# Moving batch 1's attention work by one step beside the output products of block 0 (linear attention followed by a gated feed-forward layer)

## The chip, the cores and the metric

The kernel runs on one core of one Trainium2 chip. The metric is the device time of one execution in microseconds (us). The profile of one execution gives a span that is about 1.8 us shorter than the device time of the same execution; positions inside a profile are told in us from the start of its span. The profile's short names for the engines are PE (tensor engine, matrix products), PEld (its weight loads), DVE (vector engine), ACT (scalar engine), POOL and SP (in this stretch they mainly issue loads and stores; POOL also takes a power for the norm).

## The reference

Eight batches of linear attention with 8 heads, 576 tokens and head width 64, and after it a layer with a root-mean-square norm and a gated product on all 4608 tokens:

```python
q_p = phi(q, cos_w, sin_w)           # relu(q) times cos and sin of the position, 128 wide
k_p = phi(k, cos_w, sin_w)
kv  = einsum('bhsf,bhsd->bhfd', k_p, v)
z   = sum(k_p, axis=2)
num = einsum('bhsf,bhfd->bhsd', q_p, kv)
den = einsum('bhsf,bhf->bhs', q_p, z) + 1e-06
x   = num / den                      # as [4608, 512]

xn  = x / sqrt(mean(x * x) + 1e-06) * rms_g
g   = xn @ w_gate                    # 512 -> 1536
out = (silu(g) * (xn @ w_val)) @ w_out
```

## The kernel before

The feed-forward layer is cut into blocks of 512 tokens. A block has twelve "slots" (one per 128 columns of the hidden width, each with a gate and a value product, a Silu on ACT and a product on DVE) and then its output products. The attention of batch b+1 is woven between the feed-forward products of block b. The order of instructions on each engine is the order of the program text; the kernel places every piece by hand.

This is about the end of block 0, where all four output products run side by side in four banks of PSUM, over twelve steps of the hidden width, and batch 1 is prepared between the steps. What is done for batch 1:

- **phi of k and q**: relu with a scale, half of each on DVE and half on ACT.
- **q transposes** (`q_tr`): PE transposes phi of q for 128 tokens, and DVE or ACT copies the result to SBUF.
- **k-z-v** (`kvz`): the product of phi of k with v and a column of ones (72 small products into psA), then two copies to SBUF.
- **n-d** (`nd`): numerator and denominator for 128 tokens, 8 products into psA. `nd_post` divides on DVE and so frees psA; `x_sq` (ACT) and a power on POOL give the norm's factor; `x_norm` (DVE) applies it; `tr1` transposes the result on PE, and ACT copies it. Then block 1 can use these 128 tokens.

```python
    for j in range(NJ):                                  # NJ = 9
        at(0, 8 + j // 4, "post", k_phi, V, 1, j, 0)     # DVE half, slots 8, 9, 10
        at(0, 8 + j // 4, "post", k_phi, A, 1, j, 1)     # ACT half
    for c in range(2):
        at(0, 10 + c, "post", q_phi, V, 1, c, 0)
        at(0, 10 + c, "post", q_phi, A, 1, c, 1)
    # ... slots 6 to 11 of block 0 ...
    banks0 = [psC[0][:, :], psC[1][:, :], psG[0][:, :], psG[1][:, :]]
    nd_at = {4: 0, 6: 1, 8: 2, 9: 3}
    for n in range(NNT - 2):                             # NNT = 12: steps 0 to 9
        if n == 3:
            kvz_pe(1, psA); kvz_evac(A, 1, psA, 0); kvz_evac(V, 1, psA, 1)
        if 1 <= n <= 4:
            c = n - 1
            q_tr_pe(1, c, qbank[c]); q_tr_evac(V if c < 2 else A, 1, c, qbank[c])
        if n == 0:
            ...                                          # q_phi for c = 2, 3
        if n == 1:
            v_cast(A, 1, *LOW); v_cast(V, 1, *HIGH)
        # ... loads for batch 2 ...
        if n == 7: x_norm(1, 0)
        if n == 9:
            x_norm(1, 1); tr1(0, psV[0][:, :])
        if n in nd_at:
            j = nd_at[n]
            nd_pe(1, j, psA); nd_post(1, j, psA); x_sq(1, j)
        for j in range(4):
            out_mm(0, j, n, banks0[j])
    x_norm(1, 2)
    tr1(1, psV[1][:, :])
    for j in (2, 3):
        for n in (NNT - 2, NNT - 1):
            out_mm(0, j, n, banks0[j])
    out_store(V, 0, 2, banks0[2]); out_store(A, 0, 3, banks0[3])
    for j in (0, 1):
        ...                                              # steps 10 and 11 of the others
    gval_mm(1, 0, 0, (0, 256))      # block 1's first product, into psG[0] and psV[0]
    ...                             # third and fourth xn transposes, stores, slot 1
    for n in range(2):
        gval_mm(1, n, n, (256, 512))                     # "second half" of slots 0 and 1
```

The fourth output product of step 0 goes into psG[1], which is free only when ACT has read slot 11's gate product there (its Silu). And the weights of the output product (`wo`) come in four loads of three steps; the second, for steps 3 to 5, is issued by POOL only when q of batch 1 has landed.

## Time and profile before

| | before |
|---|---|
| device time, median of 3 runs | 328.78 us (328.71 to 329.32) |
| PE busy | 318.9 us of a span of 327.9 us (97%) |
| DVE and ACT busy | 57% and 54% |
| granted PE clock | 1.00 |

The profile is of one more execution, which took 329.70 us.

PE is nearly always at work, so a reorder without a change of work can only win or lose PE's idle time. The table by windows says where that is; its columns after the window are its length, the busy time and instruction count of PE, PEld, DVE, ACT and POOL, the granted clock, the DMA share and GB/s.

```profile
38.00:62.00 24.00, 22.51 (x247) 13.70 (x246) 17.76 (x43) 17.41 (x36) 4.68 (x7) 1.00 1.06 287
62.00:327.00 265.00, 261.69 (x1839) 125.53 (x1836) 143.52 (x302) 135.87 (x280) 15.39 (x28) 1.00 0.59 143
```

In the 24 us that the change touches PE is idle for about 1.5 us by this account. A 128x512 product is recorded as 0.38 us long, but when PE is full such products start 0.216 us apart, so a record reaches about 0.16 us into the idle time behind it. The Trainium skill, "Perfetto Trace Analysis", section "Summary: the profiler window per engine type", says that the end of a PE record is an estimate; this trace agrees (0.38 against 0.216 us). So idle time is measured here from start to start: what lies between two starts, less 0.216 us for each 128x512 product in it. Here are lines of PE's timeline of the kernel before (start, duration, engine, line, operation, output and inputs, array and shape, count; in brackets the idle time by the records, and who ended it):

```profile
39.64 1.02 PE L426 MATMUL psG<-xnT,wg 128*128 128x512 bf16 x4 [0.25 <-ACT sg L435]
...
41.79 0.38 PE L446 MATMUL psG<-wo,hT 128*128 128x512 bf16 x1
43.20 0.38 PE L446 MATMUL psG<-wo,hT 128*128 128x512 bf16 x1 [1.03 <-ACT sg L435]
...
54.22 0.39 PE L412 MATMUL psV<-ident,xn 128*128 128x128 bf16 x4
54.73 0.40 PE L310 MATMUL psA<-kvzs,qpT 128*128 128x65 bf16 x8
...
56.93 1.03 PE L446 MATMUL psC<-wo,hT 128*128 128x512 bf16 x4
57.79 0.60 PE L426 MATMUL psG<-xnT,wg 128*128 128x256 bf16 x4
...
60.31 0.61 PE L426 MATMUL psG<-xnT,wg 128*128 128x256 bf16 x4
```

From start to start, slot 11 lost 0.42 us at 39.64, and the fourth product of step 0 lost 1.19 us at 43.20, both waiting for a Silu (sg). Further back there is little: the four transposes at 54.22 take 0.22 us, so the fourth n-d (54.73) waited about 0.29 us, and block 1's first product (57.79) follows the four products at 56.93 without a gap. The second half of block 1's slots starts at 60.31.

ACT's timeline of the kernel before, with the same columns, shows why the Silus are late:

```profile
37.40 1.71 ACT L209 ACTIVATE kpm<-rk,tab 128x256 bf16<-128x256 f32 x4 [1.70 <-DMA rk<-in_k_dram]
39.01 0.57 ACT L435 ACTIVATE sg<-psG 128x512 f32<-128x512 f32 x1
39.49 1.69 ACT L209 ACTIVATE kpm<-rk,tab 128x256 bf16<-128x256 f32 x4
41.08 0.58 ACT L435 ACTIVATE sg<-psG 128x512 f32<-128x512 f32 x1
41.56 0.50 ACT L209 ACTIVATE kpm<-rk,tab 128x256 bf16<-128x256 f32 x1
41.96 0.71 ACT L209 ACTIVATE qp<-rq,tab 128x512 bf16<-128x512 f32 x1
42.57 0.58 ACT L435 ACTIVATE sg<-psG 128x512 f32<-128x512 f32 x1
```

k of batch 1 lands at 37.40. From then on ACT works without a pause: nine k phis (kpm), one q phi (qp) and three Silus, and the last of these releases the product at 43.20.

### The profile page before, as it was taken

To read this page: it belongs to the slowest core of one execution; us is meant where nothing else is said; L and a number is where in the kernel's file an instruction comes from. 1 tells how busy PE (TensorE), PEld (TensorE's weight loads), DVE (VectorE), ACT (ScalarE), POOL (GpSimd) and SP (SyncE) were. 2 spreads that over 40 slices of the span, in tenths; PEclk is the share of its full clock that TensorE was granted. 3 is DMA by queue.
4 is the path that set the end of the run, shared out by engine and by line. 5 is a ranking of instruction groups with operands and counts; after the bars stand their busy time and mean duration, and the time that the engine had idled before them with its cause. 6 is when DMAs were issued, how large, how long until landed. Compare 5 with 4: busy or idle time off the path is not lost.

```text
span 327.9 us, 6438 instructions
## 1 busy us (share of the span) xinstructions
PE 318.9 (97%) x2441; PEld 161.0 (49%) x2441; DVE 185.9 (57%) x412; ACT 176.5 (54%) x366; POOL 32.1 (10%) x67
## 2 busy tenths in 40 slices
PE   7999989999999999999999999999999999999994
PEld 2488455654445444544454445444544444444442
DVE  6775577777755875578257745773577133203310
ACT  6864575875566457645654576456644233223321
POOL 1660022001100110011001100110011000000000
PEclk9999999999999999999999999999999999999999
DMA  7999999998969866975598569957621400020014
GB/s 260 217 186 224 371 165 333 325 172 198 252 187 171 209 185 170 222 206 159 186 222 193 148 187 224 197 166 210 130 49 32 130 32 0 28 102 1 0 34 96
DMA packets 80337, 53.91 MB, mean 164 GB/s; under 512 B 51377, under 2 KB 67761, under 8 KB 80306
## 3 DMA queue, kind: packets, MB, share of 16 engines
q1 hardware_dynamic: 73264, 48.64, 57.8%
q0 software_dynamic: 6880, 4.72, 10.0%
q8 instruction: 19, 0.31, 0.4%
q10 hardware_dynamic: 162, 0.13, 0.2%
q14 instruction: 12, 0.10, 0.1%
HBM read 37.75 MB, written 9.44 MB: 144 GB/s over the span
## 4 chain that ended last, share of the span: by engine, by line
PE 83%; DMA 8%; ACT 4%; DVE 1%; issue 1%; SPq 1%; POOL 0%; ACTq 0%
PE psC L446 26%; PE psG L426 24%; PE psV L426 24%; DMA rk<-in_k_dram 3%; PE psA L282 3%; DMA wv<-in_moe_w_val_dram 3%; DMA rv<-in_v_dram 2%; PE psA L310 2%; ACT kpm L209 2%; PE psG L446 1%; ACT sg L435 1%; PE psC L826 1%; PE psV L254 1%; ACT qp L209 0%; PE psA L317 0%
## 5 line engine op out<-in xcount | busy, mean ns | idle before, releaser
L441 DVE TENSOR_TENSOR hT<-psV,sg 128x512 bf16<-128x512 f32 x102 | 70.3, 689 | 97.4 <-PE psV L426 84.9
L435 ACT ACTIVATE sg<-psG 128x512 f32<-128x512 f32 x102 | 60.6, 594 | 65.9 <-PE psG L426 65.8
L426 PE MATMUL psG<-xnT,wg 128*128 128x512 bf16 (+1 forms) x368 | 92.9, 375 | 0.3 <-ACT sg L435 0.2
L426 PE MATMUL psV<-xnT,wv 128*128 128x512 bf16 (+1 forms) x368 | 92.7, 374 | 0.0
L446 PE MATMUL psC<-wo,hT 128*128 128x512 bf16 x396 | 89.6, 379 | 0.0
L426 PEld LDWEIGHTS <-wv 128*128 128x128 bf16 x416 | 40.7, 98 | 47.4
L446 PEld LDWEIGHTS <-hT 128*128 128x128 bf16 x420 | 40.2, 98 | 46.4
L426 PEld LDWEIGHTS <-wg 128*128 128x128 bf16 x416 | 38.6, 98 | 41.7 <-issue 0.5
L263 ACT COPY osb<-psC 128x512 f32<-128x512 f32 (+1 forms) x33 | 19.2, 582 | 41.0 <-PE psC L446 39.7
L380 POOL TENSOR_TENSOR rs<-ms,mhalf 128x1 f32<-128x1 f32 x36 | 19.9, 551 | 200.2 <-ACT scr L375 200.2
L387 DVE SCALAR_TENSOR_TENSOR xn<-xt,rs,gb 128x512 bf16<-128x512 f32 x36 | 26.8, 745 | 14.7 <-POOL rs L380 14.7
L375 ACT ACTIVATE scr<-xt 128x513 bf16<-128x513 f32 x36 | 22.9, 635 | 21.4 <-DVE xt L364 21.2
L209 ACT ACTIVATE kpm<-rk,tab 128x256 bf16<-128x256 f32 (+1 forms) x78 | 31.8, 477 | 3.5 <-DMA rk<-in_k_dram 3.5
L364 DVE TENSOR_TENSOR xt<-psA,rec 128x512 f32<-128x512 f32 x35 | 24.2, 691 | 1.2
L211 DVE TENSOR_SCALAR kpm<-rk,tab 128x256 bf16<-128x256 f32 (+1 forms) x84 | 22.1, 329 | 3.0 <-DMA rk<-in_k_dram 3.0
L209 ACT ACTIVATE qp<-rq,tab 128x512 bf16<-128x512 f32 x32 | 22.5, 714 | 0.2 <-DMA rq<-in_q_dram 0.2
L211 DVE TENSOR_SCALAR qp<-rq,tab 128x512 bf16<-128x512 f32 x32 | 15.1, 484 | 0.5 <-DMA rq<-in_q_dram 0.5
L310 PEld LDWEIGHTS <-qpT 128*128 128x128 bf16 x248 | 11.6, 98 | 6.7 <-issue 0.3
L310 PE MATMUL psA<-kvzs,qpT 128*128 128x65 bf16 x248 | 12.8, 194 | 0.2
L426 PE MATMUL psV<-xnt_tail,wv 128*128 128x512 bf16 x48 | 12.3, 379 | 0.0
L426 PE MATMUL psG<-xnt_tail,wg 128*128 128x512 bf16 x48 | 12.3, 379 | 0.0
L282 PEld LDWEIGHTS <-kpm 64*128 64x128 bf16 x576 | 9.9, 95 | 3.8 <-issue 2.7
(89 smaller groups left out, 168.4 us busy)
## 6 DMA issues: line engine op xcount, KB each, us to landing
out_dram<-osb SPq DMA_DIRECT2D x32, 256.0 KB, 2.5
rv<-in_v_dram SPq DMA_DIRECT2D x21, 288.0 KB, 3.2
rk<-in_k_dram SPq DMA_DIRECT2D x20, 288.0 KB, 3.5
rq<-in_q_dram SPq DMA_DIRECT2D x20, 256.0 KB, 3.4
rk<-in_k_dram SPq DMA_DIRECT2D x2, 1152.0 KB, 8.8
rq<-in_q_dram SPq DMA_DIRECT2D x2, 1024.0 KB, 11.4
rv<-in_v_dram SPq DMA_DIRECT2D x3, 576.0 KB, 10.4
wo<-in_moe_w_out_dram POOLq DMA_DIRECT2D x4, 384.0 KB, 7.0
```

The source lines that it names most:

```text
L209: nc.scalar.activation(out=out_ap, in_=in_ap, func=AF.Relu, scale=scale)
L211: eng.tensor_scalar(out=out_ap, in0=in_ap, scalar1=scale, scalar2=0.0, op0=ALU.mult, op1=ALU.max)
L282: nc.tensor.matmul(banks[c][:, r * E : (r + 1) * E], lhsT=kp_main[b][lo : lo + 64, j, r, :], rhs=vvm[b % 2][lo : lo + 64, r, j, :], start= ...
L310: nc.tensor.matmul(o[:, g, i, :], lhsT=qpT[(b, 0)][:, h, j * P : (j + 1) * P], rhs=kvz_of(b, h), start=True, stop=True,)
L364: nc.vector.tensor_tensor(out=xt[:, 0:DM].rearrange("p (b h d) -> p b h d", b=2, d=D), in0=o[:, :, :, 0:D], in1=rec[:, :, :].unsqueeze(3). ...
L375: nc.scalar.activation(out=scr[:, :], in_=xt[:, 0 : DM + 1], func=AF.Square, scale=1.0 / math.sqrt(DM), accum_out=ms[:, :],)
L380: nc.gpsimd.tensor_tensor(out=rs[:, :], in0=ms[:, :], in1=mhalf[:, :], op=ALU.pow)
L387: nc.vector.scalar_tensor_tensor(out=xn[:, :], in0=x_of[(b, j)][:, 0:DM], scalar=rs_of[(b, j)][:, :], in1=gb[:, :], op0=ALU.mult, op1=ALU. ...
L426: nc.tensor.matmul(pst[bank][:, cols[0] : cols[1]], lhsT=w[:, t, n * P : (n + 1) * P], rhs=x[:, t, cols[0] : cols[1]], start=(t == 0), sto ...
L435: nc.scalar.activation(out=sg[:, :], in_=psG[bank][:, :], func=AF.Silu)
L441: nc.vector.tensor_tensor(out=hTs[blk][:, n, :], in0=psV[bank][:, :], in1=sg[:, :], op=ALU.mult)
L446: nc.tensor.matmul(bank, lhsT=hTs[blk][:, n, j * P : (j + 1) * P], rhs=wo[:, n, :], start=(n == 0), stop=(n == NNT - 1),)
```

## The change

It takes one q phi out of the way of the last Silu, spreads the k phis as three per slot, and in return moves the q transposes and k-z-v one step later and the n-d products from steps 4, 6, 8, 9 to steps 5, 7, 9 and after the loop ("10"). No work is added or removed.

```diff
     for j in range(NJ):
-        at(0, 8 + j // 4, "post", k_phi, V, 1, j, 0)
-        at(0, 8 + j // 4, "post", k_phi, A, 1, j, 1)
-    for c in range(2):
-        at(0, 10 + c, "post", q_phi, V, 1, c, 0)
-        at(0, 10 + c, "post", q_phi, A, 1, c, 1)
+        at(0, 8 + j // 3, "post", k_phi, V, 1, j, 0)
+        at(0, 8 + j // 3, "post", k_phi, A, 1, j, 1)
+    at(0, 11, "post", q_phi, V, 1, 0, 0)
+    at(0, 11, "post", q_phi, A, 1, 0, 1)
...
-    nd_at = {4: 0, 6: 1, 8: 2, 9: 3}
+    nd_at = {5: 0, 7: 1, 9: 2}
     for n in range(NNT - 2):
-        if n == 3:
+        if n == 4:
             kvz_pe(1, psA)
...
-        if 1 <= n <= 4:
-            c = n - 1
+        if 2 <= n <= 5:
+            c = n - 2
...
         if n == 0:
-            for c in (2, 3):
+            for c in (1, 2, 3):
...
-        if n == 1:
+        if n == 2:
             v_cast(A, 1, *LOW)
...
-        if n == 7:
-            x_norm(1, 0)
         if n == 9:
-            x_norm(1, 1)
             tr1(0, psV[0][:, :])
         if n in nd_at:
             ...
+        if n in (7, 9):
+            x_norm(1, (n - 7) // 2)
         for j in range(4):
             out_mm(0, j, n, banks0[j])
+    nd_pe(1, 3, psA)
+    nd_post(1, 3, psA)
+    x_sq(1, 3)
     x_norm(1, 2)
-    tr1(1, psV[1][:, :])
     for j in (2, 3):
         for n in (NNT - 2, NNT - 1):
             out_mm(0, j, n, banks0[j])
+        if j == 2:
+            tr1(1, psV[1][:, :])
```

## The prediction

> **What bounds the kernel.** The tensor engine (PE): page part 1 shows it busy 318.9 of 327.9 us, at full granted clock (part 2). The table by windows has it busy 37.93 of 38.00 us in 62 to 100, then without a gap to 320. The change adds and removes no work; it reorders between about 34 and 62 us. All it can win or lose is PE idle time there, about 2 us in 328. A 128x512 product takes 0.216 us of PE (TensorE: Matmul & The Clock Gate, "Step-by-step", states 216 ns; the PE timeline agrees).
>
> **Idle PE time before** (PE timeline, chain of waits): 0.25 us at 39.4 and 1.03 us at 42.2, both waiting for a Silu on ACT; 0.08 us before the k-z-v product at 46.1; about 0.3 us before the fourth n-d product (54.73, waits for the normalizing multiply that frees psA); about 0.35 us near 57.8, 59.4 and 60.3. Sum 2.0 us.
>
> **What it wins.** k lands at 37.4, in slot 10. ACT then runs four k phis (0.40 us each) before the Silu of slot 9, and a q phi (0.61 us) before the Silu of slot 11, which releases psG at 43.20. PSUM — Partial Sum Buffer, "Engine vs sequencer instructions", says that the queues of ACT and DVE are strictly first in, first out; the trace agrees: the Silu of slot 9 ran at 39.01, its product was done near 36.8. With three phis per slot it starts about 38.6 (the 0.25 us gap closes), and the Silu of slot 11 has no q phi ahead: 42.0 instead of 42.57, psG free at 42.6. Gain 0.58 us. The q transposes at n=2 and k-z-v at n=4 find their inputs just ready (gaps 0 to 0.1 us).
>
> **What it loses.** n-d at 5, 7, 9 and after the loop is late. From an n-d's start to its xt done takes 1.57 us (53.11 to 54.68); x_norm adds 0.7, a PSUM copy 0.6 to 0.7.
> - tr1(0), at n=9, needs x_norm(1,0), now behind nd_post(1): ready 2.25 us after the n-d of step 7 begins; PE has 1.97 us of work: new gap 0.3 us.
> - The fourth n-d has only four output products (0.86 us) between it and the third, no longer tr1(0) too: gap 0.5 instead of 0.3 us.
> - Then PE has 2.2 us of work before block 1's first product, which needs psG[0] stored and tr1(1) copied. DVE has x_norm(1,1), nd_post(3), x_norm(1,2), then the store; ACT has x_sq(3), then the copy: done about 3.0 us after the fourth n-d starts. Gap 0.8 us instead of 0.02.
> - The gap for the last x transpose stays 0.25 us.
>
> Idle after: about 0.65+0.05+0.3+0.5+0.85+0.25 = 2.6 us, against 2.0. The win in front is paid back behind. The second half (256 columns) of block 1's first products should start about 60.9 instead of 60.31, and everything later shifts with it, PE being full.
>
> **Predicted time:** 329.3 us, range 328.3 to 330.2. Faster by over 2%: 0.005; within 2%: 0.985; slower by over 2%: 0.01.
>
> **What would show it.** Output product into psG released near 42.6; Silu of slot 9 near 38.6; PE waits for DVE or ACT before the transposes of xn at n=9, before the fourth n-d, and 0.7 us or more before block 1's first product; busy times of all engines unchanged.
>
> **What would make it wrong.** If DVE and ACT finish copies and norms sooner than I added up, the end gaps shrink and the change wins up to 0.6 us. If k lands at another time, the front gain moves. If the shift makes DVE or ACT late for batch 2's k-z-v (69.1), more is lost.

## The result

The changed kernel took 330.15 us (median of 6 runs, 329.70 to 330.50); the kernel before took 328.78 us in the same rounds and the first runs together (6 runs, 328.60 to 329.32). The ratio is 1.0038, with a 95% interval of 1.0025 to 1.0051. Ratios here are the mean time of one kernel's fast runs over that of the other's of the same rounds, so they are not quite the ratio of the medians. The change costs 0.38%, about 1.25 us: the same, by a yardstick of 2%, but clear of the noise.

The table by windows after the change, with the same columns:

```profile
38.00:62.00 24.00, 21.75 (x236) 12.71 (x238) 17.07 (x40) 16.49 (x34) 4.55 (x7) 1.00 1.08 291
62.00:328.00 266.00, 260.88 (x1816) 126.29 (x1843) 144.04 (x303) 136.27 (x281) 15.34 (x28) 1.00 0.60 142
```

PE is busy 0.76 us less in the same 24 us. Part of this is that PE's records are incomplete (some 1.5% fewer product records in this trace), so starts are the better measure. The same places in PE's timeline of the changed kernel, with the same columns:

```profile
41.16 0.38 PE L446 MATMUL psG<-wo,hT 128*128 128x512 bf16 x1
42.14 0.38 PE L446 MATMUL psG<-wo,hT 128*128 128x512 bf16 x1 [0.60 <-ACT sg L435]
...
45.52 0.59 PE L446 MATMUL psC<-wo,hT 128*128 128x512 bf16 x2 [0.25 <-DMA wo<-in_moe_w_out_dram]
...
53.77 0.40 PE L412 MATMUL psV<-ident,xn 128*128 128x128 bf16 x4 [0.15 <-DVE xn L387]
...
55.64 0.40 PE L310 MATMUL psA<-kvzs,qpT 128*128 128x65 bf16 x8 [0.36 <-DVE xt L364]
...
56.97 1.03 PE L446 MATMUL psC<-wo,hT 128*128 128x512 bf16 x4
58.64 0.60 PE L426 MATMUL psG<-xnT,wg 128*128 128x256 bf16 x4 [0.65 <-ACT xnT L263]
...
61.08 0.61 PE L426 MATMUL psG<-xnT,wg 128*128 128x256 bf16 x4
```

In front the wait for the Silu is shorter: slot 11 has no gap any more, and step 0 lost 0.76 us at 42.14. Then come waits that were not there: 0.42 us before step 3, for a load of wo; 0.31 us before the first xn transposes at 53.77; 0.53 instead of 0.29 us before the fourth n-d at 55.64; and 0.81 us before block 1's first product at 58.64. The front in ACT's timeline of the changed kernel:

```profile
36.95 1.31 ACT L209 ACTIVATE kpm<-rk,tab 128x256 bf16<-128x256 f32 x3 [1.47 <-DMA rk<-in_k_dram]
38.16 0.57 ACT L435 ACTIVATE sg<-psG 128x512 f32<-128x512 f32 x1
...
40.31 1.30 ACT L209 ACTIVATE kpm<-rk,tab 128x256 bf16<-128x256 f32 x3
41.51 0.58 ACT L435 ACTIVATE sg<-psG 128x512 f32<-128x512 f32 x1
```

k happened to land 0.45 us earlier in this execution. The Silu that releases step 0 now starts 4.56 us after k instead of 5.17: the q phi of 0.61 us is gone from in front of it. At the back, DVE's timeline of the changed kernel is full where PE waits:

```profile
54.89 0.69 DVE L364 TENSOR_TENSOR xt<-psA,rec 128x512 f32<-128x512 f32 x1
55.50 0.74 DVE L387 SCALAR_TENSOR_TENSOR xn<-xt,rs,gb 128x512 bf16<-128x512 f32 x1
...
56.59 0.69 DVE L364 TENSOR_TENSOR xt<-psA,rec 128x512 f32<-128x512 f32 x1
57.20 0.74 DVE L387 SCALAR_TENSOR_TENSOR xn<-xt,rs,gb 128x512 bf16<-128x512 f32 x1
57.86 0.68 DVE L265 COPY osb<-psG 128x512 f32<-128x512 f32 x1
```

The store of psG (osb) that block 1's first product needs stands behind the division of the fourth n-d and the third x_norm. ACT's copy of the second xn transposes (58.03 to 58.60, behind x_sq of the fourth n-d) ends still a little later, and that ended the wait.

Because k lands at a different time in every execution, three lengths describe a trace better than its span does: **R**, from the first k phi (k has landed) to the fourth product of step 0; **D**, from that product to the start of block 1's second half; and the rest, from there to the end.

| | R | D | rest |
|---|---|---|---|
| before | 43.20 - 37.40 = 5.80 | 60.31 - 43.20 = 17.11 | 327.9 - 60.31 = 267.6 |
| changed | 42.14 - 36.95 = 5.19 | 61.08 - 42.14 = 18.94 | 328.7 - 61.08 = 267.6 |

The front won 0.61 us, the back lost 1.83 us, and nothing changed afterwards. 1.83 - 0.61 = 1.22 us is what the timed runs show (1.25).

### The profile page after: what moved, and what is told of

Its sections match the earlier page's. It is cut to its first block, busy times and chain, and to the rows that moved or that the text cites. A ratio compares the mean times of both kernels' runs of the same rounds, so it can differ in the third digit from the quotient of the medians.

```text
span 328.7 us, 6404 instructions
## 1 busy us (share of the span) xinstructions
PE 317.1 (96%) x2406; PEld 160.8 (49%) x2441; DVE 186.0 (57%) x412; ACT 176.4 (54%) x366; POOL 31.9 (10%) x67
## 4 chain that ended last, share of the span: by engine, by line
PE 84%; DMA 8%; ACT 3%; DVE 3%; issue 1%; SPq 0%; ACTq 0%; POOLq 0%
PE psC L446 25%; PE psG L426 24%; PE psV L426 24%; DMA rq<-in_q_dram 4%; PE psA L282 3%; DMA rv<-in_v_dram 3%; PE psA L310 2%; DMA wo<-in_moe_w_out_dram 2%; PE psG L565 1%; PE psV L565 1%; ACT kpm L209 1%; DVE xt L364 1%; PE psC L828 1%; PE psO L565 1%; PE psG L446 1%
## 5 line engine op out<-in xcount | busy, mean ns | idle before, releaser
L426 PE MATMUL psG<-xnT,wg 128*128 128x512 bf16 (+1 forms) x352 | 90.9, 374 | 1.4 <-ACT xnT L263 0.6
L446 PE MATMUL psC<-wo,hT 128*128 128x512 bf16 x382 | 88.2, 379 | 0.9 <-DMA wo<-in_moe_w_out_dram 0.3
L446 PEld LDWEIGHTS <-hT 128*128 128x128 bf16 x420 | 40.2, 98 | 47.6 <-issue 1.3
L263 ACT COPY osb<-psC 128x512 f32<-128x512 f32 (+1 forms) x33 | 19.2, 581 | 41.0 <-PE psC L446 39.7
```

What stands on the lines that cost most here:

```text
L426: nc.tensor.matmul(pst[bank][:, cols[0] : cols[1]], lhsT=w[:, t, n * P : (n + 1) * P], rhs=x[:, t, cols[0] : cols[1]], start=(t == 0), sto ...
L446: nc.tensor.matmul(bank, lhsT=hTs[blk][:, n, j * P : (j + 1) * P], rhs=wo[:, n, :], start=(n == 0), stop=(n == NNT - 1),)
```

## The experiments

My theory: the only front win is the q phi taken out before a Silu (0.61 us); the loss is late n-d work, whose chain on DVE and ACT holds PE up at three places, and a wait for wo that the new order exposes. Rivals: that three per slot is what matters in front; that DMA landings or PE's own order set the back; that any gap closed only moves. All kernels here computed the right result. They ran on four chips, always beside the kernel before: the changed kernel again, three k phis, the earlier release of wo and the later xn transposes on the first; four k phis, the small load of wo, the order on DVE and ACT and the placement by single products on the second; the next two on the third and the last two on the fourth. The changed kernel itself was timed again only on the first. On these chips the times scattered more (the kernel before from 327.7 to 329.8 us), so that intervals are about ±0.2% wide. Effects of some tenths of a us are therefore read from R and D, each from a single trace, and the times only say whether they contradict.

### The changed kernel again

> Control: the changed kernel once more, on the chip of the runs beside it. Both theories: 1.0 to 1.4 us slower than the kernel before (ratio about 1.003 to 1.004). In its trace the gaps of PE should be there again: about 0.76 us before the fourth product of step 0, 0.4 before the first product of step 3 (wait for the second part of wo), 0.3 before the xn transposes of step 9, 0.5 before the fourth n-d, 0.8 before block 1's first product, 0.24 before its second half.

Measured: 330.13 us against 328.70, ratio 1.0041 (1.0017 to 1.0065). R was 5.19 again, D 19.27 us. The gaps were there: 0.41 us at step 0 (k landed earlier against PE), 0.75 at step 3, 0.32, 0.52, 0.82 and 0.24 us. So D of one and the same kernel differs by 0.33 us between two traces, and that is the wait at step 3. Two lines of this run, the first k phi from ACT's timeline and step 3 from PE's, give its size:

```profile
36.09 1.31 ACT L209 ACTIVATE kpm<-rk,tab 128x256 bf16<-128x256 f32 x3 [1.12 <-DMA rk<-in_k_dram]
45.00 0.59 PE L446 MATMUL psC<-wo,hT 128*128 128x512 bf16 x2 [0.58 <-DMA wo<-in_moe_w_out_dram]
```

Step 3 started 8.91 us after k here and 8.57 us after k in the first trace. Without its wait it would have started 8.16 and 8.15 us after k: ACT fixes the start of step 0 at k + 5.19, and PE's work from there is the same. So the wait at step 3 is set by how long after k the load of wo lands. It does not grow when the wait at step 0 shrinks: in three later runs with R of about 5.19 us and the same load (four k phis, later xn transposes, order on DVE and ACT) step 0 waited 0.53, 0.31 and 0.25 us, and step 3, which started 8.46 to 8.50 us after k, waited 0.35, 0.31 and 0.34 us. With R at 5.80 us, as before the change, step 3 would be due 0.61 us later and would wait 0.14 us at most (my estimate from these numbers). So 0.3 to 0.6 of the 0.61 us won in front are lost again at step 3 while that load lands when it does.

### Three k phis per slot alone

```diff
 (kernel before)
-        at(0, 8 + j // 4, "post", k_phi, V, 1, j, 0)
-        at(0, 8 + j // 4, "post", k_phi, A, 1, j, 1)
+        at(0, 8 + j // 3, "post", k_phi, V, 1, j, 0)
+        at(0, 8 + j // 3, "post", k_phi, A, 1, j, 1)
```

> The kernel before with only one part of the change: k phis three per slot instead of four, everything else as before. My theory (the fourth product of step 0 waits for the Silu of slot 11, and the same nine k phis and one q phi stand in front of that on ACT): the 0.25 us gap at slot 11 closes, the one at step 0 grows by as much; the time stays that of the kernel before within 0.15 us. Rival (every closed gap is a gain): 0.25 to 0.4 us faster than before.

Measured: 328.91 us, ratio 1.0001 (0.9975 to 1.0027). R was 41.34 - 35.53 = 5.81 us and D 17.11, as in the kernel before to 0.01 us. The profiled execution was quick (span 326.1 us) because k landed early in it, at 35.53, and 1.29 us before slot 10's product began. With such a lead slot 11 would not have waited in either order, so the trade of one gap for the other that I expected was not seen. R says that the part "three per slot" is worth nothing by itself.

### Four k phis per slot in the changed kernel

```diff
 (changed kernel)
-        at(0, 8 + j // 3, "post", k_phi, V, 1, j, 0)
-        at(0, 8 + j // 3, "post", k_phi, A, 1, j, 1)
+        at(0, 8 + j // 4, "post", k_phi, V, 1, j, 0)
+        at(0, 8 + j // 4, "post", k_phi, A, 1, j, 1)
```

> The changed kernel with k phis four per slot again, its other parts kept. My theory (the wait in front depends only on how much ACT work lies before the Silu of slot 11; the change won there because it took one q phi out, not because of three per slot): the fourth product of step 0 starts as early after the landing of k as in the changed kernel (about 5.1 us), a wait of some tenths returns at slot 11 in exchange for a smaller one at step 0; total within 0.2 us of the changed kernel. Rival (three per slot is what wins in front): 0.3 us or more slower than it.

Measured: 329.69 us, ratio 1.0031 (1.0013 to 1.0049). R was 41.36 - 36.17 = 5.19 us, as in the changed kernel, so the front win is the q phi that was taken out, not the spreading. The wait that I expected back at slot 11 did not come: k landed 0.55 us before slot 10's product began here, early enough for slot 9's Silu. D was 18.86.

### An earlier release of the second part of wo

```diff
 (changed kernel)
     w = wo_load(1)
-    tc.add_manual_dep(w.ins, gate_q.ins.name, SYNC_DEP, reason="after q of batch 1")
-    wo_load(2)
+    tc.add_manual_dep(w.ins, d.ins.name, SYNC_DEP, reason="after k of batch 1")
+    w = wo_load(2)
+    tc.add_manual_dep(w.ins, gate_q.ins.name, SYNC_DEP, reason="after q of batch 1")
```

> The changed kernel, with the load of the second part of wo released by k of batch 1 instead of q of batch 1. My theory (the reorder brought the first use of that part forward by 2.3 us, before k-z-v instead of behind it, and so exposed its landing): the 0.4 us gap at step 3 goes, 0.3 to 0.5 us faster than the changed kernel in the same rounds. Rival (that wait only stood in front of another: casts of v, done at about 45.6, are needed next, or q lands later because wo shares the DMA engines): no gain, the wait moves to k-z-v or to the q phis.

Measured: 330.06 us, ratio 1.0046 (1.0019 to 1.0073); D was 19.55 us. The expectation failed. The load was issued at 37.0 instead of 40.4, but step 3 could start only at 45.65 (9.18 us after k), where the changed kernel's started at 45.52. The line for it in the table of PE's waits of this run (waiting engine and tile, what it waited for, us in total, times, longest):

```profile
PE psC L446 <- DMA wo<-in_moe_w_out_dram: 0.9, 1, 0.9
```

It took 8.6 us from its issue instead of 5.1; q landed only at 40.2 us, so the two loads were under way together. The Trainium skill, "DMA: Bandwidth & Descriptors", section "Issuing engines are not separate DMA queues", says that loads issued by different engines share the same 16 DMA engines; this run fits that, but does not isolate it. The profiled execution also had a later wait of its own, 0.6 us for a DMA transpose of xn between 62 and 100 us, and its rest was 268.4 us; in every other trace the rest was 267.6 us.

### A small load of wo for step 3

```diff
 (changed kernel; wo_load(first step, steps) now)
-    w = wo_load(1)
+    w = wo_load(3, 1)
     tc.add_manual_dep(w.ins, gate_q.ins.name, SYNC_DEP, reason="after q of batch 1")
-    wo_load(2)
-    wo_load(3)
+    wo_load(4, 2)
+    wo_load(6, 3)
+    wo_load(9, 3)
```

(The loads of batch 2 that waited for the second load of wo now wait for the third, the one behind the small load; this holds for the later kernels with a small load too.)

> The changed kernel, with the second part of wo split: the rows of step 3 alone in a first small load (one third of the size), released as before by the landing of q, the other steps behind it. My theory (step 3 comes 2.3 us earlier in the changed order and meets the landing of a 384 KB load; an earlier release did not help, since it shared the DMA engines with q and v): the small load lands at least 1 us sooner and the wait of 0.4 to 0.8 us before step 3 goes or falls under 0.2; 0.3 to 0.6 us faster than the changed kernel. Rival (landing is set by everything queued at the engines, not by the size of this load): the wait stays.

Measured: 330.07 us, ratio 1.0035 (1.0020 to 1.0050). The small load landed 3.3 us after its issue and the wait for wo was gone, but D was still 18.77 us, only 0.17 less than the changed kernel's first trace. A line of this run's DVE timeline shows where some of it went:

```profile
42.05 1.91 DVE L211 TENSOR_SCALAR qp<-rq,tab 128x512 bf16<-128x512 f32 x4
```

The four q phis take 1.67 us in the changed kernel; here one of them took 730 ns, against a median of 475. POOL issues four loads instead of three (39.7 to 42.5), and the q transposes waited 0.39 instead of 0.13 us for the q phi. The Trainium skill, "SBUF — State Buffer", section "SBUF: two separate sides", says that DVE, in one of its two-port modes, and POOL share a pair of ports under an exclusive lock. The traces fit that in part: in the changed kernel one k phi on DVE took 508 ns while POOL issued loads, against a median of 347 ns. But in the kernel before, k phis ran beside POOL's issues and none took more than 354 ns. No run here isolates it, and no view shows in which mode a phi runs. The timed gain was not seen.

### The xn transposes behind step 9's output products

```diff
 (changed kernel)
         if n == 9:
-            tr1(0, psV[0][:, :])
 ...
             out_mm(0, j, n, banks0[j])
+    tr1(0, psV[0][:, :])
     nd_pe(1, 3, psA)
```

> The changed kernel, with the transposes of the first xn put behind the output products of step 9 instead of in front of them, so that they lie between the third and the fourth n-d as in the kernel before. My theory (late n-d work costs PE gaps): the 0.3 us gap before the transposes goes, the third n-d starts 0.5 us earlier, the gap before the fourth shrinks to 0.3; 0.4 to 0.6 us faster than the changed kernel. Rival (the back of the step is bound by the DVE and ACT chain whatever PE's order is): under 0.2 us.

Measured: 329.65 us, ratio 1.0021 (0.9996 to 1.0047), 0.48 us under the control by medians. D was 60.83 - 42.55 = 18.28 us. Of the places named, the third n-d followed its products without a gap, and the fourth waited 0.30 us, as two lines of PE's timeline show (54.87 + 0.22 to 55.39):

```profile
54.87 0.39 PE L412 MATMUL psV<-ident,xn 128*128 128x128 bf16 x4
55.39 0.40 PE L310 MATMUL psA<-kvzs,qpT 128*128 128x65 bf16 x8
```

These two gaps were 0.31 + 0.53 = 0.84 us in the changed kernel, and are 0.30 us now. The other 0.1 us of the change in D is the wait for wo, 0.30 us here.

### The order on DVE and ACT after the fourth n-d

```diff
 (changed kernel)
     nd_post(1, 3, psA)
-    x_sq(1, 3)
-    x_norm(1, 2)
     for j in (2, 3):
         ...                       # output products, tr1(1)
+    x_sq(1, 3)
     out_store(V, 0, 2, banks0[2])
+    x_norm(1, 2)
```

> The changed kernel, with only the order on DVE and ACT turned around after the fourth n-d: the store of psG before x_norm(1,2), the copy of the second xn transpose before x_sq(1,3). My theory (the 0.8 us gap before block 1's first product is those two queues): that gap falls to about 0.1 us, but x_sq(1,3) and so the last x_norm stay late, and about 0.3 us comes back before the last transpose; net 0.3 us faster than the changed kernel (0.2 to 0.6). Rival (the gap is set by PE's own products or by a DMA): the gap stays 0.8 us.

Measured: 329.42 us, ratio 1.0019 (1.0001 to 1.0037), against 1.0035 and 1.0031 for the runs beside it. D was 59.52 - 40.98 = 18.54 us. From its PE timeline:

```profile
55.72 1.03 PE L446 MATMUL psC<-wo,hT 128*128 128x512 bf16 x4
56.68 0.61 PE L426 MATMUL psG<-xnT,wg 128*128 128x256 bf16 x4
...
58.60 0.40 PE L412 MATMUL psC<-ident,xn 128*128 128x128 bf16 x4 [0.21 <-DVE xn L387]
```

The gap before block 1's first product fell from 0.81 to 0.10 us without a change of PE's order, and some of it came back before the last xn transposes. So the two queues made that gap.

### The n-d products placed by single output products

```diff
 (changed kernel)
-    nd_at = {5: 0, 7: 1, 9: 2}
+    nd_at = {19: 0, 24: 1, 30: 2, 36: 3}
 ...
         for j in range(4):
+            i = 4 * n + j
+            if i in nd_at:
+                m = nd_at[i]
+                nd_pe(1, m, psA); nd_post(1, m, psA); x_sq(1, m)
+                if m > 0:
+                    x_norm(1, m - 1)
+            if i == 34:
+                tr1(0, psV[0][:, :])
             out_mm(0, j, n, banks0[j])
 (and without the n-d, x_norm and tr1(0) lines that these replace)
```

> The changed kernel, with the four n-d placed by single output products instead of whole steps, as early as their inputs and psA allow: before products 19, 24, 30 and 36 of the 40 in the loop (changed kernel: 20, 28, 36, 40), first xn transposes before product 34. My theory (the whole loss is the late n-d work): the gaps before the xn transposes, the fourth n-d and block 1's first product fall from 0.3, 0.5 and 0.8 to at most 0.1 each; 1.3 to 1.7 us faster than the changed kernel, so 0.0 to 0.5 us faster than the kernel before; the wait for wo at step 3 remains. Rival (n-d placement doesn't matter, wo and k landings do): no gain.

Measured: 328.91 us against 328.95, ratio 0.9991 (0.9972 to 1.0010). D fell to 59.51 - 42.10 = 17.41 us, 1.5 us under the changed kernel. All of PE's waits between 30 and 62 us that the table of waits lists are now one line:

```profile
PE psC L446 <- DMA wo<-in_moe_w_out_dram: 0.4, 1, 0.4
```

The loss is undone; the wait for wo remains, as expected. (R was 5.51 us only because k landed 1.4 us before slot 10's product, so that PE and not ACT set it.)

### Both together

The same, with a small load of wo for step 3 and two loads of four steps behind it, so that POOL issues three loads as before.

```diff
 (fine placement)
-    w = wo_load(1)
+    w = wo_load(3, 1)
 ...
-    wo_load(2)
-    wo_load(3)
+    wo_load(4, 4)
+    wo_load(8, 4)
```

> The fine placement of the n-d together with a small load of wo for step 3 alone; the rest of wo in two loads of four steps, so that POOL issues no more loads than before (the split into four delayed the q phis on DVE by about 0.25 us while POOL issued). My theory: no wait for wo, no late n-d; from the landing of k to the start of block 1's second half 22.4 to 22.6 us, against 22.9 in the kernel before and in the fine placement alone and 24.1 to 24.5 in the changed kernel; 0.3 to 0.6 us faster than the kernel before. Rival (something else fills the gap, as with the split alone): 22.9 us and the time of the kernel before.

Measured: median 328.30 us against 328.66, but ratio 1.0003 (0.9974 to 1.0033), with one of its six runs at 330.51. R was 5.20 and D 58.36 - 41.33 = 17.03 us. From k to block 1's second half that is 22.23 us, 0.68 us less than before (22.91). In the trace this version beats both kernels. The times do not show a gain over the kernel before, and over the changed kernel they only suggest one: that kernel's interval (1.0025 to 1.0051) comes from other rounds and overlaps this one. The interval of the placement by single products (0.9972 to 1.0010) does not overlap it.

### Three k phis behind the last Silu

```diff
 (both together)
-        at(0, 8 + j // 3, "post", k_phi, V, 1, j, 0)
-        at(0, 8 + j // 3, "post", k_phi, A, 1, j, 1)
+        at(0, (8, 9, 11)[j // 3], "post", k_phi, V, 1, j, 0)
+        at(0, (8, 9, 11)[j // 3], "post", k_phi, A, 1, j, 1)
```

> The same, with the last three k phis moved behind the Silu of slot 11 (slots 8, 9 and 11 instead of 8, 9, 10). My theory (the fourth product of step 0 waits for what ACT has before that Silu): the product starts about 4.0 instead of 5.2 us after the landing of k, or as soon as PE gets there, and the wait goes; the q transposes come at most 0.1 us later than now after k on DVE, since its work up to there is the same, or 0.4 us earlier; 0.1 to 0.5 us faster than the run beside it. Rival (q phi and the casts of v bound the same stretch): the wait only moves to the q transposes or k-z-v, no gain.

Measured: 328.33 us, ratio 0.9996 (0.9979 to 1.0014). Step 0 lost nothing any more, but the q transposes waited, and R + D was 58.54 - 35.97 = 22.57 us, more than the 22.23 without it. The rival held: the wait only moved, as PE's timeline shows.

```profile
42.72 0.61 PE L254 MATMUL psV<-ident,qp 128*128 128x128 bf16 x8 [0.57 <-ACT qp L209]
```

### q issued only when k has landed

```diff
 (both together; and, as a second run, the kernel before)
     gate_q = load_q(1)
+    tc.add_manual_dep(gate_q.ins, d.ins.name, SYNC_DEP, reason="q after k")
```

> The fine placement with the small load of wo, and q of batch 1 issued only when k of batch 1 has landed, so that k need not share the DMA engines with it. My theory (the wait before the fourth product of step 0 is about 1.1 us less the lead by which k lands before slot 10's product begins, in all kernels with the q phi taken out): k lands 1.5 us or more before slot 10's product begins and that wait is gone; from the start of slot 10's product to the start of block 1's second half 21.0 to 21.4 us, against 21.5 in the same kernel without the gate, 22.8 before and 23.8 changed; 0.3 to 0.6 us faster than the kernel before. Rival (q, then v and wo, come later by as much as k comes earlier): the wait moves to the q transposes, to step 3 or to k-z-v, 21.5 us or more.

> The kernel before with only that gate. My theory: there the sum of the two front waits is about 1.7 us less k's lead; with k 1.5 us or more ahead it falls to 0.2 or less, so the front win that the change was after is had without moving q, k-z-v or n-d; 22.8 us from slot 10's product to block 1's second half falls to 21.3 to 21.7; the mean time falls by up to 0.5 us (less where k led by more already). Rival (q then comes too late): the first q transposes at step 1 wait instead, no gain or a loss of up to 1 us.

Measured: 332.06 us, ratio 1.0119 (1.0093 to 1.0145), and 329.86 us, ratio 1.0052 (1.0031 to 1.0072), against 328.38. Both hoped-for gains failed to come. k took as long as before (8.9 and 9.1 us from its issue; 8.8 to 9.9 us in the other traces), so it was not q that held it up, while q now landed only at 41.8 and 41.5 us (40.2 in the kernel before). In the fine placement wo then made PE wait 3.4 us in all, by the records; the rival had named step 3. In the kernel before, ACT waited for q before the q phi that stands before the Silu, as its ACT timeline shows:

```profile
41.53 0.72 ACT L209 ACTIVATE qp<-rq,tab 128x512 bf16<-128x512 f32 x1 [0.94 <-DMA rq<-in_q_dram]
```

Its R rose to 6.86 us, while D stayed at 17.11. What sets k's landing, and so much of the scatter between executions (35.5 to 37.4 us in these traces), stays open; both its issue (26.7 to 28.5 us) and the time from there vary.

## Why the prediction was right or wrong

The measured 330.15 us lies inside the predicted range, near its upper end; the direction and most of the mechanism held, but the size was too small: 329.3 predicted, that is 0.5 us, against about 1.25 us. That it still lies inside, by 0.05 us, is owed to the width of the range and not to the sum; two of the six runs took 330.46 and 330.50 us.

- **"All it can win or lose is PE idle time there"**: shown. The rest after block 1's second half was 267.6 us in all traces but one.
- **"Gain 0.58 us" in front**: right. R fell from 5.80 to 5.19 us, by 0.61. The reason given with it (nine k phis and no q phi before the Silu) was tested from both sides: three per slot alone left R at 5.81, four per slot with the q phi taken out left it at 5.19. That the slot-9 Silu starts earlier with three per slot is true and, by itself, worthless.
- **The three late n-d gaps (0.3, 0.5, 0.8)**: right, 0.31, 0.53 and 0.81 us. Reordering DVE and ACT took the third away, moving the transposes took the first two down to 0.30 together, and the fine placement took all three away.
- **"The q transposes at n=2 and k-z-v at n=4 find their inputs just ready (gaps 0 to 0.1 us)"**: this is the step that failed. The q transposes waited 0.13 us, near enough. But between them lies step 3, which I did not ask for its own input. In the kernel before it came behind k-z-v, at 47.85 us; in the new order it comes at 45.1 us, before the second part of wo lands (45.5). Its wait, 0.42 us in one trace and 0.75 in the next, is a missing term of the sum. It depends on how long after k wo lands (8.57 and 8.91 us), not on what is left to wait for at step 0.
- **The sum "2.6 us, against 2.0"**: its front terms are idle times by the records (0.25 + 1.03 us before, which are 0.42 + 1.19 from start to start; counted by starts the 0.65 after would have been 1.61 - 0.58 = 1.03). That hardly touches the difference. In D, where all is counted by starts, the idle time is 0.69 us before (0.09, 0.29, 0.07 and 0.24) and 2.54 us after (0.13, 0.42, 0.10, 0.31, 0.53, 0.81 and 0.24). The prediction's terms there give 1.95. So its terms imply a loss of 1.26 - 0.61 = 0.65 us; the 0.42 us for wo, and 0.23 instead of 0.05 us before the q transposes and k-z-v, bring it to 1.25.

Left open are why wo landed 0.34 us later after k in the second trace of the changed kernel than in the first, which makes the 0.33 us between their D, and whether the combined version is really quicker than the kernel before.

## What to carry to other kernels

When products are moved past each other on a full engine, ask of every product that comes earlier whether its own inputs are there, not only of those that the change is about: here an output product met a load of weights that had been in time before. Taking work out of the way of a wait wins only what the next wait in line leaves; count the work in front of the last release (here, nine k phis and a q phi), since spreading the same work over slots won nothing. When landing times vary between executions, measure from the landing to the place where all is equal again: R repeated to 0.01 us wherever ACT's own work set it (5.80 and 5.81, or 5.19 and 5.20), and D was 17.11 us in all three traces with the old order at the back, while the times scattered by a us. Where a second landing falls inside such a length, as wo's in D of the changed kernel, it has to be measured too.

## What the Trainium skill lacked or had wrong

- "Perfetto Trace Analysis" says that the end of a tensor-engine record is an estimate, but not by how much this hides idle time: a 128x512 product is recorded as 0.38 us and such products start 0.216 us apart, so that a gap of 0.42 us from start to start is shown as 0.25 us, and 1.19 as 1.03.
- "SBUF — State Buffer" gives the times of a load issued by POOL that waits for DVE. How much a DVE operation loses beside such a load it doesn't say (it quotes only a ratio for DVE against other POOL work): here a 128x256 k phi on DVE took 508 instead of 347 ns, and four q phis 1.91 instead of 1.67 us, beside POOL's issues (not isolated, and not in every trace).
- None of the pages that I read tells how long a load takes when it is issued into a queue of others: the same 384 KB of wo took 5.1 us behind q, and 8.6 us when it was issued 3.4 us earlier beside q and v, to land at nearly the same time.
